# Keys and values side by side in the summing matmuls of a memory-attention and FFN kernel

## The chip, the cores and the metric

The kernel runs on one core of one Trainium2 chip, in one launch. The metric is the device time of that launch in microseconds (us), as the median of repeated runs. A profile is one further execution, recorded instruction by instruction; its span runs from the first to the last instruction of the program.

The engines are named as in the profile: PE (TensorE, matrix multiplication; PEld is its loading of the stationary operand), DVE (VectorE), ACT (ScalarE), POOL (GpSimd) and SP (SyncE, which here issues every DMA).

## The reference: what is computed

For 8 batches of 8 heads, with 576 positions (S), head width 64 (D) and 32 memory slots (M), an attention goes through a small memory. Its output, 4608 rows of 512 columns, then goes through a feed-forward layer of width 2048:

```python
a = softmax(phi, axis=positions)                 # (B, H, S, M)
k_m = einsum('bhsm,bhsd->bhmd', a, k)            # sums over positions
v_m = einsum('bhsm,bhsd->bhmd', a, v)
attn = softmax(q @ k_m.T / sqrt(D), axis=slots)  # (B, H, S, M)
x = concat_heads(attn @ v_m)                     # (B * S, 512)
h = x @ w_in
out = (h * erf(softplus(h))) @ w_out
```

All inputs and outputs are fp32; the feed-forward weights arrive as 64-bit words that the kernel decodes on DVE and ACT.

## The kernel before, in words

**Folding.** The kernel never forms `x`. It multiplies `v_m` with `w_in` first (function `vw`, matmul at L637, tile `psa<-w_in,vm`), so that the first feed-forward matmul (`ffn1`, L737, `psh`) takes the attention weights as its moving operand. A batch has 16 such steps, one per 128 columns of the hidden layer, and each step is followed by softplus and erf on ACT, the product on DVE (`g_split`), and the second feed-forward matmul (`ffn2`, L796, `pso`) some steps later. `ffn1` is split into two halves of 288 positions; from the fifth step on it runs in three products of rounded and rest parts (`at_hi`, `at_lo`, `vw_hi`, `vw_lo`), `ffn2` in the same way from the seventeenth step on. Before that they run as plain fp32 matmuls, each of which shows as two records of PE in the profile.

**The summing matmuls.** `one_memory` (L571 to L627) computes `k_m` and `v_m` of one batch. The 576 positions lie in five pieces of up to 116 rows. For each of two groups of four heads (index `g`), for keys and then for values (`x`), for each piece `c` and for each head `j` of the group, a matmul at L585 (`psa<-kv,phi`) takes the 32 columns of `phi` of that head as the stationary operand and 64 columns of keys or values as the moving one. Head `j` writes the PSUM partitions from 32`j` on, so the four heads of a group stand in four separate quarters of the array's columns. From the second batch on that is one piece of PE's order with 2 x 2 x 5 x 4 = 80 matmuls; in the first batch it is split in two calls, keys and values apart. ACT then scales the sums (`kvk`, L599), PE turns them (L607), and ACT writes them to `km` and `vm`.

**Loads.** `load_kv` (L406) loads one tile of four heads, keys or values: four loads per batch of 640 KB each. They, `phi`, the queries `q` and one weight tile (`wf`) share five buffers of the pool `raw`, so a load of `q` waits for the last reader of a `kv` tile. All loads go through SP's one queue in the order in which SP issues them; in the first 60 us these are mostly the weights (`w<-w_in`, `w<-w_out`, 1024 KB each), which stand in eight buffers of the pool `wo`.

**Decoding weights.** `decode` (L425) turns a loaded weight tile into fp32 in five steps: a clamp on DVE (L432), two scalings on ACT (L438, L442), a merge (L446) and a sign step (L469) on DVE. For `w_in` the sign step writes a tile of its own, and with it the buffer is free for the next load.

**What sets the order.** All operations are first recorded with a cost, a rank and what they read and write. `Plan.order` (L128) then plays them against an estimate of every engine and emits them in the resulting order; each engine executes its list in that order, with semaphores for what really has to wait. For a load the estimate is at L219 to L222: the transfer begins 900 ns after its issue or when the one ahead has landed, goes at 250 to 385 bytes per ns, and is visible 900 ns later. `together` (L538) joins small matmuls to one piece of kind "small"; from the third batch on the sums of a batch and a `vw` piece of the batch before are one such piece.

Of the kernel before, what the change touches and what calls it, by code (L numbers as in the profile page):

```python
# [71 lines left out]
class Plan:  # L72
# [55 lines left out]
    def order(self):  # L128
# [27 lines left out]
        while len(out) < len(self.ops):  # L156
# [62 lines left out]
            if e == SP:  # L219
                begin = max(now + 900, landed)  # L220
                landed = begin + x.nbytes / (250 if x.nbytes < 1.2e5 else 340 if begin < 13000 else 385)
                x.end = landed + 900  # L222
# [17 lines left out]
def tile_memory_attention_then_erf_softplus_ffn(  # L240
    ctx: ExitStack,
    tc: tile.TileContext,
    qT: bass.AP,
    kv: bass.AP,
    phi: bass.AP,
# [23 lines left out]
    ROWS = [min(ROW, S - c * ROW) for c in range(NC)]  # L269
    assert NC == -(-S // ROW) and D < ROWS[-1]  # L270
    RAW = 5
# [45 lines left out]
    def tile_(tag, *key, shape=None, dtype=F32, pool=None):  # L317
        key = plan.tile(tag, *key)
        p, s, d = SHAPES.get(tag, (pool, shape, dtype))
        T[key] = lambda: pools[p].tile(s, d, name=key[0], tag=tag, bufs=BUFS.get(tag))  # L320
        return key
# [83 lines left out]

    def load_kv(rank, b, x, g):  # L406
        key = tile_("raw", "kv", b, x, g, shape=[P, NC, 4 * D], pool="raw")
        load(rank, P * NC * 4 * D * 4, [key],
             lambda: nc.sync.dma_start(out=get(key), in_=kv[b, x, g]))  # L409

# [160 lines left out]
    def one_memory(rank, b, part):  # L571
# [7 lines left out]
        def sums():  # L579
            for n, g in enumerate(gs):  # L580
                for y, x in enumerate(xs):
                    for c, ln in enumerate(ROWS):
                        for j in range(4):
                            h = 4 * g + j
                            nc.tensor.matmul(  # L585
                                out=get(ps)[M * j : M * (j + 1), n, y * D : (y + 1) * D],
                                lhsT=get(a)[:ln, c, h * M : (h + 1) * M],
                                rhs=get(("kv", b, x, g))[:ln, c, j * D : (j + 1) * D],
                                start=(c == 0),
                                stop=(c == NC - 1),  # L590
                            )

# [310 lines left out]
    for b in range(1, B):  # L903
# [4 lines left out]
        when(n, load_phi, at(n - 5), b)  # L908
        for x in range(2):
            for g in range(NG):  # L910
                when(n, load_kv, at(n - 4 + 2 * x + g), b, x, g)
        when(n, memories, at(n), at(n + 3), b, TOGETHER if b == 1 else [])
# [92 lines left out]
```

## Time and profile before

| | before |
|---|---|
| median of 3 runs | 722.64 us (720.65, 722.64, 722.93) |
| profiled execution | 725.49 us |
| its span, first to last instruction | 723.7 us |
| PE busy | 711.9 us (98%) |
| DVE, ACT, POOL busy | 516.4, 433.6, 103.3 us (71%, 60%, 14%) |
| DMA | 66.80 MB, mean 92 GB/s |

A row of the profile reads: line, engine, operation, written tile `<-` read tiles, the shape of the stationary operand (rows*columns) and of the moving one for PE, the count, then busy time and the mean of one in ns. In a timeline the first number is the start in us from the span's start, the second the length of the merged group, and a bracket at the end tells for how long the engine had been idle and what ended that. Matmuls overlap, so the length of one record says less than the distance from one start to the next. "PEclk" in a table of stretches is the share of the full TensorE clock that was granted there.

### The profile page before, as it was taken

What the parts mean: (1) busy time and instruction counts of PE and PEld (TensorE: products, weight loads), DVE (VectorE), ACT (ScalarE), POOL (GpSimd) and SP (SyncE); (2) the same over time, 40 slices, a digit from 0 to 9 for tenths busy, and PEclk for the clock granted to TensorE, in tenths of its full rate; (3) what the DMA queues carried; (4) which work ended last, traced back from release to release, by engine and by line L of the source; (5) the groups of instructions that cost most, each with busy time, mean ns of one, the idle gap of its engine ahead of it and who ended that gap; (6) DMA issues with size and microseconds to landing.
All of it is one profiled execution on the core that took longest, in us unless ns stands there. A gap on an engine that the chain in (4) does not pass through costs nothing.

```text
span 723.7 us, 13374 instructions
## 1 busy us (share of the span) xinstructions
PE 711.9 (98%) x5430; PEld 557.7 (77%) x5430; DVE 516.4 (71%) x950; ACT 433.6 (60%) x642; POOL 103.3 (14%) x262
## 2 busy tenths in 40 slices
PE   8999899999999999999999999999999999999997
PEld 3565555778788887888888888888888888888886
DVE  3999879877965688847974568858885378866630
ACT  4799977966644556654565545755673446664611
POOL 0022102110101111301110112111111011111110
PEclk9999999999999999999999999999999999999999
DMA  9995621171105201062102511053100300010002
GB/s 320 405 404 176 211 81 36 51 254 37 37 1 203 82 33 38 4 236 63 38 1 83 183 54 37 1 205 99 37 1 1 124 16 1 1 45 15 1 0 74
DMA packets 27054, 66.80 MB, mean 92 GB/s; under 512 B 2032, under 2 KB 10224, under 8 KB 25968
## 3 DMA queue, kind: packets, MB, share of 16 engines
q1 hardware_dynamic: 26992, 65.94, 25.9%
q8 instruction: 43, 0.70, 0.4%
q14 instruction: 19, 0.16, 0.1%
HBM read 56.49 MB, written 9.44 MB: 91 GB/s over the span
## 4 chain that ended last, share of the span: by engine, by line
PE 89%; ACT 6%; DMA 3%; SPq 1%; issue 0%; DVE 0%
PE pso L796 48%; PE psh L737 26%; PE psr L796 6%; PE psa L637 6%; DMA q<-qT 3%; PE psa L585 2%; ACT w L442 1%; ACT w L438 1%; ACT e L760 1%; SPq L409 1%; ACT e L765 1%; ACT L760 1%; ACT h L753 0%; PE idle L368 0%; PE psa L607 0%
## 5 line engine op out<-in xcount | busy, mean ns | idle before, releaser
L796 PE MATMUL pso<-wo,g_hi 128*128 128x512 f32 x896 | 281.1, 395 | 0.0
L760 ACT ACTIVATE e<-h 128x576 f32<-128x576 f32 x128 | 87.4, 686 | 178.6 <-DVE h L752 176.6
L796 PEld LDWEIGHTS pso<-wo,g_hi 128*128 128x128 f32 x896 | 160.3, 188 | 42.2 <-issue 15.1
L796 PE MATMUL pso<-wo,g_lo 128*128 128x512 f32 x448 | 176.1, 393 | 0.0
L752 DVE COPY h<-psh 128x288 f32<-128x288 f32 x240 | 107.0, 451 | 48.9 <-PE psh L737 47.2
L737 PE MATMUL psh<-at_hi,vw_hi 128*128 128x288 f32 x496 | 113.6, 310 | 0.0
L792 POOL CAST rest<-g_hi 128x64 fp32r<-128x64 f32 x112 | 49.7, 443 | 406.0 <-DVE g_hi L787 392.2
L737 PE MATMUL psh<-at_lo,vw_hi 128*128 128x288 f32 x496 | 106.6, 297 | 0.0
L737 PE MATMUL psh<-at_hi,vw_lo 128*128 128x288 f32 x496 | 106.3, 296 | 0.0
L785 DVE TENSOR_TENSOR e<-e,h 128x576 f32<-128x576 f32 x112 | 82.8, 751 | 30.3 <-ACT e L765 30.1
L737 PEld LDWEIGHTS psh<-at_hi,vw_hi 128*128 128x128 f32 x496 | 86.5, 189 | 22.1 <-issue 8.2
L796 PEld LDWEIGHTS pso<-wo,g_lo 128*128 128x128 f32 x448 | 84.1, 188 | 19.2
L788 DVE TENSOR_TENSOR g_lo<-e,g_hi 128x576 fp32r<-128x576 f32 x112 | 86.4, 772 | 6.2
L787 DVE CAST g_hi<-e 128x576 fp32r<-128x576 f32 x112 | 50.6, 453 | 46.0 <-PE pso L796 43.4
L765 ACT ACTIVATE e<-e 128x576 f32<-128x576 f32 x128 | 80.3, 675 | 0.4
L737 PEld LDWEIGHTS psh<-at_hi,vw_lo 128*128 128x128 f32 x496 | 80.2, 189 | 0.0
L737 PEld LDWEIGHTS psh<-at_lo,vw_hi 128*128 128x128 f32 x496 | 79.4, 188 | 0.0
L359 DVE TENSOR_TENSOR vw_lo<-psa,vw_hi 128x512 fp32r<-128x512 f32 (+1 forms) x68 | 41.3, 632 | 16.9 <-ACT vw_hi L357 16.7
L796 PE MATMUL pso<-w,g 128*128 128x512 f32 x112 | 52.9, 604 | 0.0
L796 PE MATMUL psr<-wo,rest 128*128 128x512 f32 x192 | 49.0, 391 | 0.0
L357 ACT ACTIVATE vw_hi<-psa 128x512 fp32r<-128x512 f32 (+1 forms) x68 | 34.9, 554 | 22.7 <-PE psa L637 22.7
L792 POOL CAST rest<-g_lo 128x64 fp32r<-128x64 f32 x112 | 34.0, 304 | 90.6 <-DVE g_lo L788 86.4
(80 smaller groups left out, 690.6 us busy)
## 6 DMA issues: line engine op xcount, KB each, us to landing
kv<-kv SPq DMA_DIRECT2D x32, 640.0 KB, 8.0
q<-qT SPq DMA_DIRECT2D x16, 576.0 KB, 6.0
w<-w_in SPq DMA_DIRECT2D x8, 1024.0 KB, 14.2
w<-w_out SPq DMA_DIRECT2D x8, 1024.0 KB, 14.7
out<-ot SPq DMA_DIRECT2D x32, 256.0 KB, 2.1
phiT<-phiT SPq DMA_DIRECT2D x16, 288.0 KB, 3.0
phi<-phi SPq DMA_DIRECT2D x7, 640.0 KB, 7.6
out<-ot SPq DMA_DIRECT2D x8, 128.0 KB, 2.3
```

The costliest lines, as they stand in the source:

```text
L357: lambda: nc.scalar.activation(get_hi(), get_src(), AF.Identity))
L359: lambda: nc.vector.tensor_tensor(out=get_lo(), in0=get_src(), in1=get_hi().bitcast(F32), op=ALU.subtract))
L637: nc.tensor.matmul(out=get(ps[par])[p * M : (p + 1) * M, :], lhsT=w[rows, p, :], rhs=x[rows, p, :], start=True, stop=True,)
L737: nc.tensor.matmul(out=get(ps), lhsT=x[:, g, k % 4 * P : (k % 4 + 1) * P], rhs=y[:, g, :], start=(n + g == 0), stop=(n == len(parts) - 1 a ...
L752: lambda: nc.vector.tensor_copy(out=keep(), in_=get(ps)),
L760: last[:] = [op(ACT, on_act(S), rank, [("h", i)], [e], lambda: nc.scalar.activation(get(e), get(("h", i)), AF.Softplus), kind="softplus", ...
L765: last[:] = [op(ACT, on_act(S), rank, [e], [e], lambda: nc.scalar.activation(get(e), get(e), AF.Erf), kind="erf", edge=edge, after=last)]
L785: op(DVE, on_dve(S), rank, [e, h], [e], lambda: nc.vector.tensor_tensor(out=get(e), in0=get(e), in1=get(h), op=ALU.mult))
L787: op(DVE, on_dve(S, 1), rank, [e], [hi], lambda: nc.vector.tensor_copy(out=get(hi), in_=get(e)))
L788: op(DVE, on_dve(S), rank, [e, hi], [lo], lambda: nc.vector.tensor_tensor(out=get(lo), in0=get(e), in1=get(hi).bitcast(F32), op=ALU.subtract))
L792: lambda x=x, y=y: nc.gpsimd.tensor_copy(out=rest[:, k, x, cols], in_=get(y)[:, NT * P :]))
L796: nc.tensor.matmul(out=o, lhsT=y, rhs=z, start=(start and n == 0), stop=(stop and n == len(parts) - 1))
```

## The change

It has two parts, which are built in together.

**Layout and loops.** Of the first batch, keys and values stay in separate tiles of four heads (`kv_0`). From the second batch on the host lays keys and values of each head side by side, 64 columns of keys and then 64 of values, and a tile holds two heads instead of four heads of one kind. A tile is as large as before, 640 KB, and a batch has four of them as before. In `one_memory` the loop over keys and values is gone: one matmul takes the 128 columns of a head, so 2 x 5 x 4 = 40 matmuls do what 80 did, each twice as wide. The planned cost of the piece is the same as before. The four loads of a batch are recorded with the groups outside and the pairs inside, so that both tiles of the first four heads come first. With the loop over pieces now outside that over heads, both tiles of a group are read until the last of its 20 matmuls.

**Planned loads.** The planner lets a transfer begin 1400 ns after its issue instead of 900.

```diff
             if e == SP:
-                begin = max(now + 900, landed)
+                begin = max(now + 1400, landed)
                 landed = begin + x.nbytes / (250 if x.nbytes < 1.2e5 else 340 if begin < 13000 else 385)
...
     def load_kv(rank, b, x, g):
         key = tile_("raw", "kv", b, x, g, shape=[P, NC, 4 * D], pool="raw")
-        load(rank, P * NC * 4 * D * 4, [key],
-             lambda: nc.sync.dma_start(out=get(key), in_=kv[b, x, g]))
+        src = kv[b - 1, 2 * g + x] if b else kv_0[x, g]
+        load(rank, P * NC * 4 * D * 4, [key], lambda: nc.sync.dma_start(out=get(key), in_=src))
...
             for n, g in enumerate(gs):
-                for y, x in enumerate(xs):
-                    for c, ln in enumerate(ROWS):
-                        for j in range(4):
-                            h = 4 * g + j
-                            nc.tensor.matmul(
-                                out=get(ps)[M * j : M * (j + 1), n, y * D : (y + 1) * D],
-                                lhsT=get(a)[:ln, c, h * M : (h + 1) * M],
-                                rhs=get(("kv", b, x, g))[:ln, c, j * D : (j + 1) * D],
-                                start=(c == 0),
-                                stop=(c == NC - 1),
-                            )
+                for c, ln in enumerate(ROWS):
+                    for j in range(4):
+                        h, w = 4 * g + j, n_x * D
+                        kv_of, at_ = (("kv", b, j // 2, g), j % 2) if b else (("kv", b, xs[0], g), j)
+                        nc.tensor.matmul(
+                            out=get(ps)[M * j : M * (j + 1), n, :w],
+                            lhsT=get(a)[:ln, c, h * M : (h + 1) * M],
+                            rhs=get(kv_of)[:ln, c, at_ * w : (at_ + 1) * w],
+                            start=(c == 0),
+                            stop=(c == NC - 1),
+                        )
...
-        for x in range(2):
-            for g in range(NG):
-                when(n, load_kv, at(n - 4 + 2 * x + g), b, x, g)
+        for g in range(NG):
+            for x in range(2):
+                when(n, load_kv, at(n - 4 + 2 * g + x), b, x, g)
...
-    kv = np.stack([k, v]).reshape(2, B, 2, H // 2, S, D).transpose(1, 0, 2, 4, 3, 5)
+    kv = np.stack([k, v])
...
-        "kv": rows(kv.reshape(B, 2, 2, S, H // 2 * D)),
+        "kv_0": rows(kv[:, 0].reshape(2, 2, H // 2, S, D).swapaxes(2, 3).reshape(2, 2, S, H // 2 * D)),
+        "kv": rows(kv[:, 1:].reshape(2, B - 1, H // 2, 2, S, D).transpose(1, 2, 4, 3, 0, 5)
+                   .reshape(B - 1, H // 2, S, 4 * D)),
```

Few places of the engines' orders differ, the first of them in the second batch. (The changed kernel's lines are 1 to 2 higher: L585 became L587, L637 L639, L737 L739, L796 L798.) The first place is PE where the second batch is prepared. `pso<-w,g` is an `ffn2` matmul in plain fp32, `psa<-w_in_103,vm_98` a `vw` piece of the first batch. Before:

```order
L737 MATMUL psh<-at_hi,vw_lo 128x288 x2
L796 MATMUL pso<-w,g 128x512
L637 MATMUL psa<-w_in_103,vm_98 32x256 x8
L796 MATMUL pso<-w,g 128x512 x3
L737 MATMUL psh<-at_hi,vw_hi 128x288 x2
```

In the changed kernel:

```order
L739 MATMUL psh<-at_lo,vw_hi 128x288 x2
L739 MATMUL psh<-at_hi,vw_lo 128x288 x2
L639 MATMUL psa<-w_in_103,vm_98 32x256 x8
L798 MATMUL pso<-w,g 128x512 x4
L739 MATMUL psh<-at_hi,vw_hi 128x288 x2
```

The `vw` piece stands ahead of one `ffn2` matmul that it stood behind. Twelve `ffn1` matmuls later, at the sums of the second batch (`psa<-kv,phi`), PE before:

```order
L737 MATMUL psh<-at_hi,vw_lo 128x288 x2
L796 MATMUL pso<-w,g 128x512 x2
L585 MATMUL psa<-kv,phi 32x64 x80
L637 MATMUL psa<-w_in_103,vm_98 32x256 x8
L796 MATMUL pso<-w,g 128x512
L607 MATMUL psa<-ident,kvk 128x128 x4
```

And now:

```order
L739 MATMUL psh<-at_hi,vw_lo 128x288 x2
L798 MATMUL pso<-w,g 128x512
L587 MATMUL psa<-kv,phi 32x128 x40
L639 MATMUL psa<-w_in_103,vm_98 32x256 x8
L798 MATMUL pso<-w,g 128x512 x2
L609 MATMUL psa<-ident,kvk 128x128 x4
```

The 80 matmuls became 40 of twice the width, and one `ffn2` matmul went from ahead of them to behind them. Between the `vw` piece and the sums stand as many `ffn2` matmuls as before, five.

The third place is DVE over both of these stretches, before. `w` is a weight tile being decoded, with the sign step of `w_in_103` at L469; `pmx` the maxima of the third batch's `phi`, `h` a copy of an `ffn1` half out of PSUM, `vw_lo` the rest part of a `vw` piece.

```order
L494 TENSOR_REDUCE pmx<-phiT 128x1 x2
L446 SCALAR_TENSOR_TENSOR w<-w 128x1024
L752 COPY h<-psh 128x288
L469 SCALAR_TENSOR_TENSOR w_in_103<-w 128x4x256
L446 SCALAR_TENSOR_TENSOR w<-w 128x1024
L496 TENSOR_SCALAR pmx<-pmx 128x1
L469 SCALAR_TENSOR_TENSOR w<-w 128x1024
L359 TENSOR_TENSOR vw_lo<-psa,vw_hi 128x256 x2
L496 TENSOR_SCALAR pmx<-pmx 128x1
L446 SCALAR_TENSOR_TENSOR w<-w 128x1024
L432 TENSOR_SCALAR w<-w 128x1024
L469 SCALAR_TENSOR_TENSOR w_in_103<-w 128x4x256
```

And in the changed kernel:

```order
L496 TENSOR_REDUCE pmx<-phiT 128x1
L448 SCALAR_TENSOR_TENSOR w<-w 128x1024
L754 COPY h<-psh 128x288
L471 SCALAR_TENSOR_TENSOR w_in_103<-w 128x4x256
L448 SCALAR_TENSOR_TENSOR w<-w 128x1024
L754 COPY h<-psh 128x288
L471 SCALAR_TENSOR_TENSOR w<-w 128x1024
L360 TENSOR_TENSOR vw_lo<-psa,vw_hi 128x256 x2
L496 TENSOR_REDUCE pmx<-phiT 128x1
L448 SCALAR_TENSOR_TENSOR w<-w 128x1024
L498 TENSOR_SCALAR pmx<-pmx 128x1
L471 SCALAR_TENSOR_TENSOR w_in_103<-w 128x4x256
```

One of the two maxima left the place ahead of the first sign step of `w_in_103`, and the clamp of another weight (L432) left the place ahead of the second; one copy of `h` came in from ACT. SP issues its loads in the same sequence of kinds as before. The other places move `ffn2` steps by one past neighbours: the sums of the third batch stand one `ffn2` step of three matmuls later than before, and in three places near the ends of later batches an `ffn2` step changes place with `ffn1` halves.

More of the change, by code (lines that the diff above doesn't have):

```diff
@@ L243, in tile_memory_attention_then_erf_softplus_ffn @@
     qT: bass.AP,
+    kv_0: bass.AP,
     kv: bass.AP,
@@ L269, in tile_memory_attention_then_erf_softplus_ffn @@
     ROWS = [min(ROW, S - c * ROW) for c in range(NC)]
-    assert NC == -(-S // ROW) and D < ROWS[-1]
+    assert NC == -(-S // ROW) and D < ROWS[-1] and H == 8
     RAW = 5
```

## The prediction, made before the changed kernel ran

> **What bounds the kernel now.** I read the page's first part, then the stretches with the granted clock, then PE's waits, and at last PE's timeline around each wait. The page:
>
> ```profile
> PE 711.9 (98%) x5430; PEld 557.7 (77%) x5430; DVE 516.4 (71%) x950; ACT 433.6 (60%) x642; POOL 103.3 (14%) x262
> q8 instruction: 43, 0.70, 0.4%
> ```
>
> The stretches (start:end; then busy time and count of PE, PEld, DVE, ACT, POOL; granted clock, DMA share, GB/s):
>
> ```profile
> 88.30:90.17 1.87, 0.16 (x3) 0.04 (x2) 1.18 (x3) 1.86 (x4) 0.56 (x1) 1.00 1.05 394
> 91.60:95.40 3.80, 3.80 (x25) 1.85 (x23) 2.94 (x6) 1.00 (x2) 0.56 (x2) 0.58 0.75 261
> 95.40:149.00 53.60, 53.60 (x257) 34.58 (x250) 46.85 (x75) 44.72 (x62) 10.11 (x18) 1.00 0.16 52
> 154.00:700.00 546.00, 545.71 (x4112) 454.36 (x4101) 384.58 (x737) 302.69 (x445) 77.84 (x210) 1.00 0.18 60
> ```
>
> After 154 us PE never stops (545.71 of 546.00 us), while DVE is busy for 70% of that and ACT for 55%. There only less work on PE shortens the program, and moving an `ffn2` step past `ffn1` halves costs nothing, hidden by that slack. The waits that an order can change lie ahead of 154 us. Two matter.
>
> **The sums.** PE's timeline at the fourth batch's sums, and the groups of the sums and of the 128-column turns:
>
> ```profile
> 222.50 2.45 PE L585 MATMUL psa<-kv,phi 116*32 116x64 f32 x160
> 224.88 1.09 PE L637 MATMUL psa<-w_in,vm 64*32 64x512 f32 x16
> 225.90 0.50 PE L796 MATMUL pso<-wo,g_hi 128*128 128x512 f32 x1
> 228.99 0.60 PE L607 MATMUL psa<-ident,kvk 128*128 128x128 f32 x4
> L585 PE MATMUL psa<-kv,phi 116*32 116x64 f32 x1024 | 19.0, 220 | 1.4 <-DMA kv<-kv 1.4
> L607 PE MATMUL psa<-ident,kvk 128*128 128x128 f32 x32 | 5.4, 281 | 0.0
> ```
>
> The 80 matmuls are 160 records, two passes each. The piece takes 224.88 - 222.50 = 2.38 us; with 0.22 us for the last record's length (220 ns), the pace is (2.45 - 0.22) / 159 = 14.0 ns per record, or 56 ns for the four that stand side by side in the array's quarters. Is this the time of 64 columns, or of issuing an instruction? The turns stream 128 columns and follow each other at (0.60 - 0.28) / 3 = 107 ns (0.28 us is one record's length, 281 ns in its group). Half of it is 53 ns. So the columns set the pace, with some 3 ns per pass on top. Forty matmuls are 20 rounds of four records at 107 to 110 ns, 2.14 to 2.20 us, against 40 rounds x 56 = 2.24. That saves 0.04 to 0.10 us per piece, and there are seven. I take **0.5 us**; the bounds are 0 (a round exactly twice as long) and 7 x (2.38 - 2.14) = 1.7 us, if the piece's ends shrink too.
>
> [...]
>
> The layout itself I cost at nothing: the loads are as large and as many, and PE's 1.4 us of waiting for `kv` tiles, told by the last row but one above, is these two waits of the first batch, whose loads don't change:
>
> ```profile
> 8.73 0.77 PE L585 MATMUL psa<-kv,phi 116*32 116x64 f32 x40 [0.54 <-DMA kv<-kv]
> 10.36 0.77 PE L585 MATMUL psa<-kv,phi 116*32 116x64 f32 x40 [0.86 <-DMA kv<-kv]
> ```
>
> No later sums waited for a tile: the loads are ahead of them, which covers their new order. Without that lead a tile would cost its lateness at the sums.
>
> **The gap in the third batch's sums.** PE, and the chain of waits there:
>
> ```profile
> 149.58 2.46 PE L585 MATMUL psa<-kv,phi 116*32 116x64 f32 x160
> 151.97 0.61 PE L637 MATMUL psa<-w_in,vm 64*32 64x512 f32 x1
> 153.37 1.09 PE L637 MATMUL psa<-w_in,vm 64*32 64x512 f32 x15 [0.79 <-issue]
> 154.39 0.74 PE L796 MATMUL pso<-wo,g_hi 128*128 128x512 f32 x2
> 152.58 0.79 issue
> q8 instruction: 1, 0.02, 4.1%
> ```
>
> The `vw` piece behind the sums takes 154.39 - 151.97 = 2.42 us here, and 225.90 - 224.88 = 1.02 us a batch later: 1.40 us lost after its first record, to nothing that the profile shows as a wait. The last row is from the DMA view of 150.5 to 152.5 us: one piece of instructions was on its way. The page has 43 of them with 0.70 MB, 16 KB each; PE's 10,860 matmuls and loads of weights make 253 per piece. Sums and `vw` piece together are 320 + 32 = 352 instructions in 2.4 us, more than one piece, so PE can run dry. In the changed kernel they are 160 + 32 = 192, less than a piece. I take the whole **1.4 us**, bounds 0 and 1.4.
>
> [...]
>
> **The wait for q.** PE, SP and DVE in the second batch:
>
> ```profile
> 74.21 1.02 PE L796 MATMUL pso<-w,g 128*128 128x512 f32 x2
> 75.39 0.67 PE L637 MATMUL psa<-w_in,vm 64*32 64x256 f32 x16 [0.16 <-ACT e L760]
> 80.25 1.88 PE L796 MATMUL pso<-w,g 128*128 128x512 f32 x4
> 82.06 2.46 PE L585 MATMUL psa<-kv,phi 116*32 116x64 f32 x160
> 88.03 0.43 PE L737 MATMUL psh<-at_hi,vw_lo 128*128 128x288 f32 x2
> 90.17 0.84 PE L637 MATMUL psa<-q,km 64*32 64x288 f32 x16 [1.71 <-DMA q<-qT]
> 81.86 0.33 SPq L391 DMA_DIRECT2D w<-w_out  x1
> 82.89 0.94 SPq L414 DMA_DIRECT2D q<-qT  x2
> 82.89 7.14 DMA q<-qT
> q<-qT SPq DMA_DIRECT2D x1, 576.0 KB, 4.4
> 71.21 1.40 DVE L494 TENSOR_REDUCE pmx<-phiT 128x1 f32<-128x576 f32 x2
> 74.03 1.21 DVE L469 SCALAR_TENSOR_TENSOR w_in<-w 128x1024 int32<-128x1024 int32 x1
> 79.95 0.70 DVE L432 TENSOR_SCALAR w<-w 128x1024 f32<-128x1024 f32 x1 [0.37 <-DMA w<-w_out]
> 80.56 1.22 DVE L469 SCALAR_TENSOR_TENSOR w_in<-w 128x1024 int32<-128x1024 int32 x1
> 76.54 0.69 ACT L357 ACTIVATE vw_hi<-psa 128x256 fp32r<-128x256 f32 x2
> 77.06 1.24 ACT L442 ACTIVATE w<-w 128x1024 f32<-128x1024 f32 x1
> 80.18 1.27 ACT L515 ACTIVATE phi<-phi 116x1280 f32<-116x1280 f32 x1
> ```
>
> PE is through with `ffn1` at 88.03 + 2 x 0.13 = 88.29 and gets `q` at 90.17: 1.88 us idle. `q` takes 7.14 us to land, but 4.4 us when nothing is ahead of it (the DMA view of its issue at 223.4 us). Ahead of it is a `w_out` load, issued at 81.86, when the sign step of `w_in` ends (80.56 + 1.22 = 81.78) and frees its buffer. That step stands behind a clamp that waits 0.37 us for a load and takes 0.61 us. The change puts the clamp behind it and a copy of 0.4 us ahead: the `w_out` load goes out 0.37 + 0.61 - 0.4, with a small step gone some 0.7 us earlier, and `q` lands 0.7 us earlier, since the queue is what it waits for.
>
> Does PE come to it later? The first sign step loses one maximum of 0.70 us ahead of it, so the `vw` piece starts about 0.6 us earlier, at 74.8, though PE then idles 0.6 us ahead of it instead of 0.3: the `ffn2` matmul of 74.21, which filled that time, now follows. ACT rounds this piece ahead of a weight's scaling instead of behind it (76.54, ended by 77.2); it can do so from about 75.6, when it used to copy `h`, so the scaling of 77.06 and the exponentials at 80.18 keep their times. The sums follow the `vw` piece 82.06 - 75.39 = 6.67 us later as before, at 81.5, or 81.6 when the exponentials (80.18 + 1.27) are through. PE's way from there to `q` is 88.29 - 82.06 = 6.23 us, plus 0.9 for the `ffn2` matmul put there (two took 82.06 - 80.25 = 1.81), less 0.07 for the sums: 88.7. `q`'s first buffer is free after 18 of 40 matmuls instead of 20 of 80, 0.4 us later in the piece, which the earlier start gives back. So `q` lands at 90.03 - 0.7 and the piece starts at 89.5: **0.7 us** gained, bounds 0 and 90.17 - 88.7 = 1.5. What is late next is nothing on PE: 95.40 to 149 is filled.
>
> **The clock behind it.** Between 91.60 and 95.40 us the clock is 0.58: 3.80 x 0.42 = 1.6 us lost, right behind the idle 1.88 us, and nowhere else in the quoted stretches. With 0.8 us idle I expect full clock. But one profile can't say how often the timed runs had the drop; they spread over 2.3 us, more than it costs. I take half, **0.8 us**, bounds 0 and 1.6.
>
> **The sum.** 0.5 + 1.4 + 0.7 + 0.8 = 3.4 us. The profiled execution took 725.49 (span 723.7 and 1.8 around it), which would become 722.1; the median of the runs is 2.85 us lower, so I take 722.64 - 3.4 = **719.2 us**.
>
> **Rivals.**
> *One: only the sums shrink.* DVE meets another wait (its merges wait for ACT), `w_out` goes out as before, idle time and clock stay, and the gap moves elsewhere: 722.1 us. For it: moved steps elsewhere in a full order change nothing. Against: the clamp's wait is in the trace. Chance 0.16.
> *Two: the gap at 152 us stays*, because it isn't instructions: 719.2 + 1.4 = 720.6. For it: one gap in seven batches. Against: no wait ends there, and a piece was in flight. Chance 0.20.
> *Three: issue sets the sums' pace.* Then 80 records take 80 x 14.0 = 1.1 us, 1.2 less in each of seven: 711.5. Against it, the turns' 107 ns. Chance 0.03.
> *Four, slower: the `vw` piece put forward waits.* If the first sign step ends at 75.24 as before, PE idles 0.9 us more at 74.2; if `w_out` then goes out no earlier, `q` comes 0.4 us later by its buffer and the idle time grows to about 3.2 us in two parts. From about 1.9 us on the clock drops, and a second stretch of 1.6 us is lost: 722.64 - 0.5 + 1.3 + 1.6 = 725.0, with the gap unchanged. Chance 0.06.
>
> **How the numbers follow.** The forecast has 0.55. A measurement of this kernel tells about 0.3% from no change, 2.2 us, so faster means below 720.5: 0.85 of the forecast, half of rival two and rival three, 0.60. Slower by that, above 724.8: most of rival four, 0.05. The rest, 0.35, is no change. The range starts where all terms have their upper bounds but the sums' (722.64 - 0.5 - 1.4 - 1.5 - 1.6 = 717.6) and reaches to 722.3, past rival one.
>
> **What would show it.** The sums' piece 2.3 us from start to start with 80 records; the `vw` piece behind the third batch's sums in one group of 16; instructions in 38 pieces; the `w_out` load ahead of `q` issued near 81.2, PE's `q` piece near 89.5, and a granted clock of 1.00 behind it. Wrong would be: sums of 1.2 us or of more than 2.4; the gap still there; a longer bracket at the `q` piece.

## The result and the profile after

The changed kernel takes **718.97 us** (median of 5 runs, 717.89 to 719.05) against 722.64 us before: 0.9943 of the time, 95% interval 0.9923 to 0.9963. A second measurement on another occasion gave 0.9950 (0.9937 to 0.9964). Its profiled execution took 717.89 us, with a span of 716.1 us. The prediction was 719.2 us.

The page of the changed kernel, engines and instruction pieces:

```profile
PE 708.0 (99%) x4870; PEld 555.7 (78%) x4870; DVE 516.9 (72%) x951; ACT 432.8 (60%) x641; POOL 105.8 (15%) x262
q8 instruction: 38, 0.62, 0.4%
```

PE's timeline after the change, at the sums of the third batch and at those of the fifth:

```profile
145.70 2.40 PE L587 MATMUL psa<-kv,phi 116*32 116x128 f32 x80
148.03 1.09 PE L639 MATMUL psa<-w_in,vm 64*32 64x512 f32 x16
149.05 0.74 PE L798 MATMUL pso<-wo,g_hi 128*128 128x512 f32 x2
...
298.90 2.40 PE L587 MATMUL psa<-kv,phi 116*32 116x128 f32 x80
301.23 1.09 PE L639 MATMUL psa<-w_in,vm 64*32 64x512 f32 x16
302.25 0.53 PE L739 MATMUL psh<-at_hi,vw_hi 128*128 128x288 f32 x2
```

The sums take 148.03 - 145.70 = 2.33 us from start to start, 2.38 before. The `vw` piece behind them is one group of 16 and takes 1.02 us, where it took 2.42 us before: that gap is gone. The fifth batch holds something that the prediction had overlooked. The same place in the kernel before, and its view of PE's waits (line and releaser, then us in total, times, longest):

```profile
304.99 2.45 PE L585 MATMUL psa<-kv,phi 116*32 116x64 f32 x160
307.37 1.06 PE L637 MATMUL psa<-w_in,vm 64*32 64x512 f32 x7
308.72 1.07 PE L637 MATMUL psa<-w_in,vm 64*32 64x512 f32 x9 [0.29 <-issue]
309.71 0.53 PE L737 MATMUL psh<-at_hi,vw_hi 128*128 128x288 f32 x2
```

```profile
PE psa L637 <- issue: 1.1, 2, 0.8
```

There was a second gap: 309.71 - 307.37 = 2.34 us instead of 1.02, 1.32 us lost, though the bracket shows only 0.29 us of it, because the group of seven ahead is drawn with 1.06 us, up to 308.43, which covers the rest. The waits said "2 times". The changed kernel has neither gap.

The wait for `q` in the second batch, PE after the change:

```profile
86.16 0.43 PE L739 MATMUL psh<-at_hi,vw_lo 128*128 128x288 f32 x2
87.07 0.92 PE L639 MATMUL psa<-q,km 64*32 64x288 f32 x16 [0.48 <-DMA q<-qT]
```

0.48 us of idle time by the bracket, 1.71 before.

Where the time went is read from the starts of PE's pieces in its timelines. The last two columns are a second profile of each kernel, told of below:

| start of PE's piece, us | before | after | before, again | after, again |
|---|---|---|---|---|
| third `w_in,vm` piece | 43.32 | 41.79 | 43.45 | 43.73 |
| second batch's sums | 82.06 | 79.58 | 82.20 | 81.54 |
| second batch's first `q` piece | 90.17 | 87.07 | 90.80 | 88.92 |
| a `w_in,vm` piece past the third batch's sums | 182.64 | 176.63 | 181.41 | 178.40 |
| a `w_in,vm` piece past the fifth batch's sums | 331.19 | 323.73 | 329.78 | 325.81 |
| end of PE | 719.25 | 711.46 | 718.03 | 713.53 |

The first pair differs by 7.8 us at the end, twice what the medians differ by. 1.53 us of it arise in the first 43 us, where both kernels do the same, and 1.7 us are the half-clock stretch that the prediction quoted (3.41 us at 0.50, from 91.38 to 94.79 us). In the second pair no half-clock stretch falls behind the first row. It differs by 4.50 us at the end, or by 4.78 us counted from the first row, where the changed kernel is 0.28 us later (a half-clock stretch at 11.4 us of its profile lies ahead of that row).

### The profile page after: what moved, and what is told of

The parts are those of the page before. It is cut to its first block, busy times and chain, and to the rows that moved or that the text cites. A ratio compares the mean times of both kernels' runs of the same rounds, so it can differ in the third digit from the quotient of the medians.

```text
span 716.1 us, 12256 instructions
## 1 busy us (share of the span) xinstructions
PE 708.0 (99%) x4870; PEld 555.7 (78%) x4870; DVE 516.9 (72%) x951; ACT 432.8 (60%) x641; POOL 105.8 (15%) x262
## 4 chain that ended last, share of the span: by engine, by line
PE 89%; ACT 6%; DMA 3%; SPq 1%; DVE 0%; issue 0%
PE pso L798 49%; PE psh L739 26%; PE psr L798 6%; PE psa L639 5%; DMA q<-qT 3%; PE psa L587 2%; ACT w L444 1%; ACT w L440 1%; ACT e L762 1%; ACT e L767 1%; ACT L762 1%; ACT h L755 0%; SPq L411 0%; PE idle L369 0%; PE psa L609 0%
## 5 line engine op out<-in xcount | busy, mean ns | idle before, releaser
L798 PE MATMUL pso<-wo,g_hi 128*128 128x512 f32 x896 | 280.8, 395 | 0.0
L798 PEld LDWEIGHTS pso<-wo,g_hi 128*128 128x128 f32 x896 | 160.2, 188 | 42.1 <-issue 15.1
L798 PE MATMUL pso<-wo,g_lo 128*128 128x512 f32 x448 | 175.9, 393 | 0.0
L739 PE MATMUL psh<-at_hi,vw_hi 128*128 128x288 f32 x496 | 112.8, 309 | 0.0
L739 PE MATMUL psh<-at_lo,vw_hi 128*128 128x288 f32 x496 | 106.2, 296 | 0.0
L739 PE MATMUL psh<-at_hi,vw_lo 128*128 128x288 f32 x496 | 105.9, 295 | 0.0
L739 PEld LDWEIGHTS psh<-at_hi,vw_hi 128*128 128x128 f32 x496 | 86.1, 188 | 21.7 <-issue 7.6
L798 PEld LDWEIGHTS pso<-wo,g_lo 128*128 128x128 f32 x448 | 84.1, 188 | 19.5
L739 PEld LDWEIGHTS psh<-at_hi,vw_lo 128*128 128x128 f32 x496 | 79.8, 189 | 0.0
L739 PEld LDWEIGHTS psh<-at_lo,vw_hi 128*128 128x128 f32 x496 | 79.0, 188 | 0.0
L798 PE MATMUL pso<-w,g 128*128 128x512 f32 x112 | 52.2, 599 | 0.0
L798 PE MATMUL psr<-wo,rest 128*128 128x512 f32 x192 | 49.0, 390 | 0.0
L794 POOL CAST rest<-g_lo 128x64 fp32r<-128x64 f32 x112 | 34.2, 305 | 87.9 <-DVE g_lo L790 85.9
```

Of the source, the lines that this page charges most:

```text
L739: nc.tensor.matmul(out=get(ps), lhsT=x[:, g, k % 4 * P : (k % 4 + 1) * P], rhs=y[:, g, :], start=(n + g == 0), stop=(n == len(parts) - 1 a ...
L794: lambda x=x, y=y: nc.gpsimd.tensor_copy(out=rest[:, k, x, cols], in_=get(y)[:, NT * P :]))
L798: nc.tensor.matmul(out=o, lhsT=y, rhs=z, start=(start and n == 0), stop=(stop and n == len(parts) - 1))
```

## The experiments

### Both kernels once more, and each part of the change alone

Four kernels ran beside the kernel before. The first is that kernel unchanged. The second has the planner's number alone:

```diff
-                begin = max(now + 900, landed)
+                begin = max(now + 1400, landed)
```

The third is the changed kernel with that line set back. The fourth is the changed kernel, in its order and with its layout, with each wide matmul issued as two:

```diff
-                for c, ln in enumerate(ROWS):
-                    for j in range(4):
+                for y in range(n_x):
+                    for c, ln in enumerate(ROWS):
+                        for j in range(4):
...
-                            out=get(ps)[M * j : M * (j + 1), n, :w],
+                                out=get(ps)[M * j : M * (j + 1), n, y * D : (y + 1) * D],
...
-                            rhs=get(kv_of)[:ln, c, at_ * w : (at_ + 1) * w],
+                                rhs=get(kv_of)[:ln, c, at_ * w + y * D : at_ * w + (y + 1) * D],
```

What was expected of the kernel before, again:

> The kernel before, unchanged, for a second profile of it. Theory (the two gaps belong to the program, the start and the clock to the single execution): the vw piece behind the third batch's sums again takes 2.4 us and that behind the fifth batch's 2.3 us instead of 1.02; the start of the w_in,vm piece that stood at 43.32 us moves by up to 1.5 us, since in the changed kernel it stood at 41.79 with the same work ahead of it; the idle time ahead of the second batch's q piece is 1.3 to 1.9 us. Rival (the changed kernel's start is 1.5 us earlier because the first batch's keys and values come from a tensor of their own): that piece stands at 43.3 again, within 0.3 us. The half-clock stretch of 1.6 us behind the q piece: if the idle time sets it, it is there again; if it is a matter of the single execution, it may be gone.

Of the planner's number alone:

> The kernel before with the planner's 1400 in place of 900 and nothing else: the changed order with 80 matmuls of 64 columns per sums. Theory: both gaps stay (2.4 and 2.3 us for the vw pieces behind the third and the fifth batch's sums, 43 pieces of instructions), the idle time ahead of the second batch's q piece falls from 1.7 to about 0.5 us: 0.6 to 1.2 us less than before, 721.4 to 722.0, and up to 1.6 us less again if the timed runs of before had the half-clock stretch. Rival (the gap at 152 us is not a matter of instructions, the moved ffn2 step or loads took it away): both gaps are gone here too, 719.3.

Of the wide sums in the old order:

> The changed kernel with the planner's 900: 40 matmuls of 128 columns per sums in the old order. Theory: both gaps gone (1.02 us for the vw pieces, 38 pieces of instructions) and 0.05 us less in each of seven sums: 2.7 + 0.35 = 3.1 us less than before, 719.6; the idle time ahead of the second batch's q piece stays at 1.3 to 1.9 us. Rival (gaps not a matter of instructions): they stay, 0.35 us less than before, 722.3.

Of narrow sums in the new order and layout:

> The changed kernel, its layout, loads and order, but each summing matmul of 128 columns issued as two of 64, so that sums and vw piece are 352 instructions again. Theory: the gaps are back behind the third and the fifth batch's sums (the stream up to there has as many instructions as before, within 6), each sums takes 2.38 us: 2.7 + 0.35 = 3.1 us more than the changed kernel, 722.0. Rival (the gaps belonged to the order or to the loads): no gap, 719.3.

Measured, as ratios to the kernel before with 95% intervals:

| | narrow sums | wide sums |
|---|---|---|
| old order | 0.9993 (0.9975 to 1.0011) | 0.9950 (0.9934 to 0.9966) |
| new order | **1.0061** (1.0044 to 1.0079) | 0.9943 (0.9923 to 0.9963) |

Narrow sums in the new order with the new layout have 1.0063 (1.0047 to 1.0079), the same as with the old layout: the layout itself costs and gives nothing, the number of matmuls does. The wide sums give the whole gain, also in the old order. The planner's number, for which 1.5 us had been forecast, gives nothing that can be told beside wide sums with PE's instructions as they lie here, and with narrow sums it makes the kernel **slower** by 0.6%, which neither theory nor rival had.

The kernel before, again, in PE's timeline, behind the third and the fifth batch's sums:

```profile
151.05 0.61 PE L637 MATMUL psa<-w_in,vm 64*32 64x512 f32 x1
152.12 1.09 PE L637 MATMUL psa<-w_in,vm 64*32 64x512 f32 x15 [0.46 <-issue]
153.14 0.74 PE L796 MATMUL pso<-wo,g_hi 128*128 128x512 f32 x2
...
306.14 2.19 PE L637 MATMUL psa<-w_in,vm 64*32 64x512 f32 x16
308.26 0.54 PE L737 MATMUL psh<-at_hi,vw_hi 128*128 128x288 f32 x2
```

Both gaps are there again, 1.07 and 1.10 us. Its start is at 43.45 us, that of the wide sums in the old order at 43.27: the early start of the changed kernel's first profile was that execution's own.

The clock, in stretches of the first and of the second profile of the kernel before (start:end; busy time and count of PE, PEld, DVE, ACT, POOL; granted clock, DMA share, GB/s):

```profile
88.00:91.30 3.30, 1.59 (x21) 0.85 (x20) 1.70 (x5) 3.27 (x5) 0.78 (x2) 1.00 1.05 403
91.40:94.80 3.40, 3.40 (x16) 1.86 (x22) 2.54 (x6) 1.20 (x2) 0.56 (x2) 0.50 0.88 312
```

```profile
88.00:91.30 3.30, 1.03 (x21) 0.62 (x19) 1.55 (x4) 3.25 (x6) 0.86 (x3) 1.00 1.04 384
91.40:94.80 3.40, 3.40 (x33) 1.69 (x26) 3.09 (x6) 1.45 (x3) 0.56 (x2) 1.00 0.94 334
```

The second has the longer idle time (2.27 us by its bracket, against 1.71) and no half clock behind it. So the length of the wait alone doesn't decide.

And this is what the new order does to narrow sums. PE in the second batch with the planner's number alone:

```profile
80.75 2.15 PE L585 MATMUL psa<-kv,phi 116*32 116x64 f32 x137
86.64 0.79 PE L585 MATMUL psa<-kv,phi 116*32 116x64 f32 x23 [3.75 <-issue]
87.36 1.11 PE L637 MATMUL psa<-w_in,vm 64*32 64x256 f32 x16
```

The sums stop at the 137th of 160 records for 3.75 us, and again nothing ended the wait that the profile shows. Narrow sums in the new layout do the same (4.03 us). In the third batch both have a gap of 1.6 us, in the fifth one of 1.2.

### What decides where a gap comes

Counting PE's matmuls, loads of weights and semaphore instructions from the program's start puts the gaps in a row. In the kernel before they begin at records 2496 and 5056, with the planner's number at 1472, 2496 and 5056. Each of these is 256 n + 448 (n = 4, 8, 18). The 16 KB pieces of instructions in the DMA records come once per 256 such records, in quiet stretches soonest when PE is at record 256 n + 152. From 448 - 152 = 296 I estimate that a piece is asked for some 300 records ahead of its use. No record shows the asking; a time that an expectation gives for it is an estimate too, that of PE's record 256 n + 148 (record 1428, at 83.62 us, in the kernel before). In the kernel before, the sums use up 300 records in 2.07 us at the fastest; in the changed kernel no 300 records in a row take less than 10 us behind the first 40 us. From the record at 256 n + 148 to PE's going on, the four gaps of the kernel before's two profiles took 3.65, 3.51, 3.31 and 3.30 us.

If that is the cause, instructions that do nothing, put in front, move the gaps. The kernel issues matmuls on zeros during PE's first waits; some of these were issued as four of 128 columns instead of one of 512, so that each adds six instructions (a load of weights and a matmul, three times) and no columns:

```diff
-            nc.tensor.matmul(
-                out=idle[0].rearrange("p (n c) -> p n c", c=P), lhsT=zeros,
-                rhs=zeros.unsqueeze(1).to_broadcast([P, DM // P, P]), start=True, stop=True,
-            )
+            n_parts = 4 if len(idle) <= 11 else 1
+            idle.append(None)
+            w = DM // P // n_parts
+            for y in range(n_parts):
+                nc.tensor.matmul(
+                    out=idle[0].rearrange("p (n c) -> p n c", c=P)[:, y * w : (y + 1) * w], lhsT=zeros,
+                    rhs=zeros.unsqueeze(1).to_broadcast([P, w, P]), start=True, stop=True,
+                )
```

With 11 of them, 66 instructions, the kernel before was expected so:

> The kernel before with 66 more small instructions on PE in its first microseconds (11 of the matmuls that fill PE's waits there are issued as four of 128 columns each), the order otherwise unchanged. Theory: PE's instructions come in pieces of 256; a piece is asked for 300 instructions before it is needed, and it takes 3.3 to 3.7 us; PE stands still where those 300 are used up faster. With 66 more ahead the boundary moves to other places: the gaps behind the third and the fifth batch's sums go (1.02 us for these vw pieces), and gaps of 1.2 to 1.4 us come behind or in the fourth and the eighth batch's sums, near 224 and 561 us; the time stays within 0.3% of before. Rival (the gaps belong to these two places: their loads, tiles or buffers): they stay in the third and the fifth batch, and none comes elsewhere.

Measured: 1.0054 (1.0034 to 1.0073). PE's timeline at the fourth, fifth and eighth batch's sums:

```profile
225.06 1.04 PE L641 MATMUL psa<-w_in,vm 64*32 64x512 f32 x2
226.30 1.09 PE L641 MATMUL psa<-w_in,vm 64*32 64x512 f32 x14 [0.19 <-issue]
227.31 0.73 PE L800 MATMUL pso<-wo,g_hi 128*128 128x512 f32 x2
...
308.75 1.09 PE L641 MATMUL psa<-w_in,vm 64*32 64x512 f32 x16
309.77 0.40 PE L741 MATMUL psh<-at_hi,vw_hi 128*128 128x288 f32 x1
...
559.66 2.34 PE L589 MATMUL psa<-kv,phi 116*32 116x64 f32 x152
563.75 0.32 PE L589 MATMUL psa<-kv,phi 112*32 112x64 f32 x8 [1.75 <-issue]
564.00 1.09 PE L641 MATMUL psa<-w_in,vm 64*32 64x512 f32 x16
```

The fifth batch's gap is gone (1.02 us), and gaps stand in the fourth (1.23 us lost) and the eighth (564.00 - 559.66 = 4.34 us instead of 2.38, 1.96 lost), the two batches that had been named. So the gaps belong to PE's instruction count, not to the place, its tiles or its loads. The time was missed, +0.5% where no change was forecast: the eighth batch's gap is longer than 1.4 us, 0.58 us stay in the third, and this profile has a half-clock stretch behind `q`. None of its six timed executions has a mean granted clock above 0.998, so that stretch is probably in most of them.

With 22 split, 132 instructions, in two kernels:

> The order of the changed kernel with the narrow sums, as the run with the planner alone, and 132 more small instructions on PE in the first microseconds. Theory: none of the boundaries then falls into the second, third or fifth batch's sums; the stall of 3.75 us in the second, the 1.6 us in the third and the 1.2 us in the fifth are gone, one gap of about 1.3 us comes at the seventh batch's sums near 472 us. 3.75 + 1.6 + 1.2 - 1.3 = 5.2 us less than with the planner alone, and about 1.7 us more where that run had a half-clock stretch: 0.2 to 0.5% faster than before. Rival (the 3.75 us belong to the moved order: a tile or a load that the sums wait for): the stall in the second batch stays, and the kernel stays 0.4 to 0.6% slower than before.

> The changed kernel with the same 132 instructions more. Theory: with wide sums no place in the program uses up 300 instructions in less than 3.7 us, so the boundary may lie anywhere: no gap of 0.6 us or more behind 60 us, 0.994 to 0.995 of before like the changed kernel. Rival (the changed kernel was only lucky with where its boundaries fall): a gap of 1 us or more somewhere, 0.996 or more.

The new order with narrow sums goes from 1.0061 to **0.9960** (0.9945 to 0.9975), by nothing but 132 instructions that compute nothing. Its sums in the second and in the seventh batch:

```profile
81.21 2.46 PE L589 MATMUL psa<-kv,phi 116*32 116x64 f32 x160
83.59 0.66 PE L641 MATMUL psa<-w_in,vm 64*32 64x256 f32 x16
...
468.32 2.46 PE L589 MATMUL psa<-kv,phi 116*32 116x64 f32 x160
472.32 1.09 PE L641 MATMUL psa<-w_in,vm 64*32 64x512 f32 x16 [1.54 <-issue]
```

The stall of the second batch is gone, and the one gap stands at the seventh batch's sums as forecast (472.32 - 468.32 is 1.62 us more than 2.38). The changed kernel with the same 132 has 0.9939 (0.9922 to 0.9956). No wait in its view of PE's waits is put down to `issue`: with wide sums no stall came with the pieces ending at this place either.

### Why 3.75 us in the second batch

The gaps of the kernel before cost 1.1 to 1.4 us, this one 3.75. At 80.3 us a `w_out` load is issued; it was left out:

```diff
+                if c == NPR - 1:
+                    nc.gpsimd.memset(t.bitcast(F32), 0.0)
+                    return
                 nc.sync.dma_start(
                     out=t.rearrange("p (r d) -> p r d", d=DM), in_=w_out[:, 2 * c : 2 * c + 2]
                 )
```

> The run with the planner alone, but the last w_out load, which is issued near 80.3 us, is left out, and its buffer is filled with zeros by POOL instead (so one eighth of w_out counts as zero). Theory (the piece of instructions asked for at 78.2 us came 8.5 us later instead of 3.5 because it stood behind this load in the DMA engines): the piece is there by 82.2 us and the stall in the second batch's sums falls from 3.75 us to under 0.6 us; 3.2 to 5 us less than with the planner alone. The gaps in the third and the fifth batch stay. Rival (the stall's length has nothing to do with loads): it stays at 3 us or more.

Measured: 1.0000 (0.9985 to 1.0016), 4.7 us less than the planner's number alone by the medians (723.80 and 728.53 us). Not all of that is the stall: the two profiled executions, each with one half-clock stretch, are only 1.6 us apart (725.39 and 727.02 us), and the mean granted clock of the timed ones is 0.998 to 1.000 here and 0.991 to 0.998 there. And the stall is 1.89 us, not under 0.6:

```profile
80.44 2.15 PE L588 MATMUL psa<-kv,phi 116*32 116x64 f32 x137
84.48 0.54 PE L588 MATMUL psa<-kv,phi 116*32 116x64 f32 x23 [1.89 <-issue]
```

The piece went into the DMA engines at 81.57 us instead of 84.31, 1.1 us behind the start of the sums instead of 3.6, so the load did hold it up by some 2.4 us. It didn't go at 79 us, though, when the engines had nothing to do. My guess was that it had not been asked for by then, which no record shows. In the order before, the second batch's sums stand four records later in the stream (they begin at record 1202, here at 1198), and their piece came at 79.75 us, ahead of them. That gave the last experiment: six instructions more, one split matmul.

> The run with the planner alone (narrow sums in the new order) with 6 more small instructions on PE in its first microseconds: one of the matmuls that fill PE's waits is issued as four. In the order before, the second batch's sums stood 4 instructions later in PE's stream than in the new one, and the piece of instructions that they need came at 79.8 us, ahead of them; in the new order it came at 84.3 us, and PE stood still for 3.75 us. Theory (the place in the stream that asks for the piece lies just behind the sums' first instruction in the new order, so that it is asked for when the sums start and then waits behind a load; a few instructions earlier it is asked for before them): with 6 more the piece comes ahead of the sums, near 79 us, and the stall in the second batch is gone; the gaps in the third and the fifth batch stay (1.2 to 1.6 us each), since their boundaries move by 6 of 256 only. 0.999 to 1.002 of before, where the planner alone had 1.006. Rival (the stall belongs to the new order and its loads): it stays, 1.005 or more.

Measured: **0.9973** (0.9959 to 0.9987), against 1.0061 without them. PE in the second batch, and the DMA queues from 77.9 to 79.9 us:

```profile
80.47 2.45 PE L589 MATMUL psa<-kv,phi 116*32 116x64 f32 x160
82.85 0.66 PE L641 MATMUL psa<-w_in,vm 64*32 64x256 f32 x16
83.44 1.98 PE L800 MATMUL pso<-w,g 128*128 128x512 f32 x4
```

```profile
q8 instruction: 1, 0.02, 4.0%
```

The piece came at 78.3 us and the stall is gone, while the third batch keeps its gap. Six empty instructions are worth 0.9% here, 6.7 us by the medians of the two occasions. The clock has a part in that beside the stall: its mean is 0.999 or more in all twelve executions, and 0.998 or less in all six without the six instructions. With the sums' first instruction at record 1024 + 174, the piece came behind their start, by 3.6 us and, without the load, by 1.1 us; with it at 1024 + 178 (the order before) and at 1024 + 180 (six more), the piece came 2.3 and 2.2 us ahead of their start. Why these few records decide isn't shown: the packet can be seen, the request can't.

### What shortened the wait for q

Wide sums in the old order had 0.55 us of idle time ahead of the `q` piece, where 1.3 to 1.9 had been expected, though their `w_out` load went out at 82.26 us, later than before (81.86). So the order, to which the prediction had put the gain, isn't needed for a short wait. In the two profiles of before a piece of instructions passed through the DMA engines at 87.9 and 87.4 us, while `q` was on its way; with wide sums in the old order none did. 132 instructions bring one back among these loads (22 matmuls split, as above):

> Wide sums in the old order (the run with the new layout alone) with 132 more small instructions on PE in its first microseconds. In the old order with wide sums no piece of instructions was asked for between 62 and 89 us, and q landed 2.2 us behind the w_out load ahead of it; in the two profiles of before a piece was asked for at 83.6 to 83.8 us, its 16 KB came at 87.4 to 87.9 us, and q landed 3.5 and 4.1 us behind w_out. With 132 more, a piece is asked for at 83.7 us again. Theory (the wait for q in before was 1 to 1.9 us longer because a piece of instructions came through the DMA engines while w_out and q did): w_out and q together are 1 us or more later again, the idle time ahead of the second batch's q piece goes from 0.55 us back to 1.3 us or more; no gap of 0.6 us behind it; 0.996 to 0.998 of before. Rival (the wide sums shortened the wait for q in another way): idle time of 0.4 to 0.8 us, 0.994 to 0.996 of before.

> The changed kernel, unchanged, for a second profile and beside the run with wide sums in the old order. Theory (its start at 41.8 us for the third w_in,vm piece was the single execution's): the piece stands at 42.6 to 43.6 us, as in the other profiles, and the span is 716 to 718.5 us; no gap of 0.6 us behind 60 us. It has 0.993 to 0.995 of before; wide sums in the old order had 0.995, so the order's share is at most 0.2%.

PE's `q` piece, and the loads issued and queues at work from 83.5 to 88.3 us, in the wide kernel of the old order without and then with the 132 (of a load: KB, then median us to landing):

```profile
89.21 0.84 PE L639 MATMUL psa<-q,km 64*32 64x288 f32 x16 [0.55 <-DVE h L754]
```

```profile
q<-qT SPq DMA_DIRECT2D x2, 576.0 KB, 5.8
```

```profile
89.89 0.84 PE L643 MATMUL psa<-q,km 64*32 64x288 f32 x16 [1.68 <-DMA q<-qT]
```

```profile
q8 instruction: 1, 0.02, 1.2%
...
q<-qT SPq DMA_DIRECT2D x2, 576.0 KB, 7.0
```

The idle time is 1.68 us again. From the issue of `w_out` to the start of the `q` piece it takes 89.89 - 82.02 = 7.87 us with the piece of instructions among the loads, and 89.21 - 82.26 = 6.95 without: 0.9 us more. The other 0.2 us of the difference are PE's, which comes to `q` that much sooner after the issue. The piece is one packet, and it took 0.9 us too (1.2% of 16 engines' 4.8 us).

In the changed kernel, though, a piece passed among these loads as well, at 83.4 us and in its second profile at 85.3 us, and the wait is short all the same. Its second profile, in DVE, SP, the DMA queues from 83.5 to 88.3 us, and PE:

```profile
79.74 1.23 DVE L471 SCALAR_TENSOR_TENSOR w_in<-w 128x1024 int32<-128x1024 int32 x1
81.03 0.33 SPq L392 DMA_DIRECT2D w<-w_out  x1
81.67 0.69 DVE L434 TENSOR_SCALAR w<-w 128x1024 f32<-128x1024 f32 x1
...
q8 instruction: 1, 0.02, 1.3%
...
88.92 0.84 PE L639 MATMUL psa<-q,km 64*32 64x288 f32 x16 [0.37 <-DVE g L776]
```

`w_out` goes out when the sign step ends (79.74 + 1.23 = 80.97 us), with the clamp behind it, as the prediction had it. The parts of the wait in ten profiles, all in us, read from the starts of the sums, of the `w_out` load and of the `q` piece with its bracket (in the other three the stall in the sums let `q` land before PE came to it):

| profiles | `w_out` issued before the sums start | sums' start to PE being ready for `q` | `w_out` issued to `q` piece | idle |
|---|---|---|---|---|
| old order, a piece among the loads: before, again, with 66, wide with 132 | 0.20, 0.27, -1.05, 0.05 | 6.39, 6.33, 6.51, 6.13 | 8.31, 8.87, 7.87, 7.87 | 1.71, 2.27, 2.42, 1.68 |
| old order, no piece: wide | 0.27 | 6.13 | 6.95 | 0.55 |
| new order, a piece: changed, again, with 132 | 0.48, 0.51, 0.49 | 7.01, 7.02, 6.98 | 7.97, 7.89, 7.76 | 0.48, 0.37, 0.28 |
| new order, a piece, narrow: with 132, with 6 | 0.48, 0.49 | 7.05, 7.05 | 7.70, 8.88 | 0.17, 1.34 |

The idle time is the third number less the first two. In all ten the piece starts 0.13 to 0.14 us behind `q`'s landing, also where the bracket names DVE. The first two numbers, which go mostly with the order, give the new order 0.9 us in either pair of before and changed (0.28 + 0.62 and 0.24 + 0.69). The third gives these pairs 0.34 and 0.98 us, with a piece among the loads on both sides, at another place; without a piece it is 0.8 to 1.9 us lower than with one. So the order or a missing piece is enough for a short wait, and in the changed kernel no piece is missing.

Over the whole the wide kernel of the old order with the 132 has 0.9990 (0.9976 to 1.0003), slower than the 0.996 to 0.998 expected. One reason is a wait that nobody had forecast, in ACT's and PE's timelines:

```profile
317.17 0.60 ACT L845 ACTIVATE ot<-pso 128x512 f32<-128x512 f32 x1 [1.35 <-DMA out<-ot]
...
317.82 0.72 PE L802 MATMUL pso<-wo,g_hi 128*128 128x512 f32 x2 [1.03 <-ACT ot L845]
```

ACT there waits 1.35 us for a store of the output to land before it frees a PSUM buffer, and PE 1.03 us for ACT. A piece of instructions passed at 305.84 us, among the loads queued ahead of this store, and the store took 8.2 us to land; without the 132 the pieces came at 301.92 and 313.59 us, and it took 5.6 us. That the piece delayed the store fits, but wasn't tried by itself.

The changed kernel, again, has 0.9950 and 0.37 us ahead of `q`; its third `w_in,vm` piece stood at 43.73 us, 0.1 us beyond what was expected. At 0.9950 against 0.9950 for wide sums in the old order, the order's part can't be told from nothing. With the 132 instructions it can: 0.9939 (0.9922 to 0.9956) in the new order against 0.9990 in the old, on two occasions. So what the order is worth depends on where the pieces of instructions fall.

## Why the prediction came out

The number was right, 719.2 against 718.97 us, and the causes of its terms hold in the main. The sizes don't: the gaps and the wait for `q` were put too low and the clock too high for a pair of profiles without the half-clock stretch, so that the agreement to 0.2 us is in part luck.

**Sums, 0.5 us.** Measured 2.38 to 2.33 us in each of seven, 0.35 us: mis-sized slightly. The reason holds: 80 records at (2.40 - 0.27) / 79 = 27 ns are 108 ns per four, with 107 to 110 forecast, against 56 ns for 64 columns, so columns set the pace. Rival three, issue at 14 ns, would have gained 1.2 us per piece.

**The gap, 1.4 us.** The cause, instructions, is shown by the moved gaps, and rival two, that it stays, is out. Two things in this step were wrong. The rule was not that 352 instructions are more than one piece and 192 are less: sums and `vw` piece were 352 instructions in all seven batches and only two had a gap. What goes with a gap is how fast 300 records pass (2.07 us at the fastest in the kernel before, over 10 us in the changed one) and where they lie against 256 n + 448. And there were two gaps, so that the term should have been 2.7 us by that profile; by the second one it is 2.2. "After 154 us PE never stops", read from 545.71 busy us of 546.00, missed the second, because the 1.06 us with which the seven matmuls ahead are drawn cover all but 0.29 us of it. The line `issue: 1.1, 2, 0.8` had it.

Of the 43 pieces of instructions in the kernel before, 41 came without such a gap. Where PE stood still, it cost 0.6 to 4 us here.

**The wait for q, 0.7 us.** The idle time fell by 1.23 us in the first pair and 1.90 in the second, and the step behind it, that the `w_out` load goes out 0.7 us earlier and `q` lands earlier with it, holds in the changed kernel. Counted from the third `w_in,vm` piece, `w_out` goes out 1.2 us earlier in both pairs, so that the step was sized too small. What the prediction left out is that the time in the queue isn't fixed: from the issue of `w_out` to the `q` piece it went from 8.31 to 7.97 us and from 8.87 to 7.89, and it was 6.95 us where no piece of instructions passed.

**The clock, 0.8 us.** The stretch is gone in the changed kernel's profile (1.00 from 60 to 700 us), 1.7 us. But rival four's "From about 1.9 us on the clock drops" doesn't hold: 2.27 us of idle time in the second profile of the kernel before had no half clock behind it (1.00 from 91.4 to 94.8 us). Of 74 executions of the kernel before that were timed beside these runs, 21 had a mean granted clock of 0.997 or less, and their median is 2.4 us above that of the others (725.4 and 723.0 us). 21/74 of 2.4 us is 0.7 us, near the half that was taken. It is a lower count: the profile of the planner's number alone has one such stretch and a mean of 0.998.

**The sum.** In the second pair of profiles, of the 4.78 us counted from the third `w_in,vm` piece, the `q` piece starts 2.16 us earlier, the gaps are 1.07 + 1.10 us, and six more sums 0.30: 4.6 us. Against this the forecast of 3.4 us has 0.8 too little for the gaps, 1.4 too little up to `q`, 0.8 too much for the clock and 0.2 for the sums. The medians differ by 3.4 to 3.7 us, less than these profiles; why is open, though both profiled executions of the kernel before (725.49 and 724.27 us) lie above the median of their occasion. What was missed altogether is that the planner's number, taken alone, costs 4.4 us. Rival four had the sign and the batch, but another mechanism, and in the change as a whole the wide sums take it away.

## What to carry to other kernels

Where an engine works through hundreds of short instructions in a few microseconds, look for idle time put down to "issue" and count the instructions up to it: here the remainder was the same at every gap (256 n + 448), instructions that compute nothing moved the gaps, and halving the instructions there took away 2.2 to 2.7 us of gaps beside 0.35 us of execution time. When an edit of the order gains or loses a few us, run it once more with some empty instructions ahead, since six of them moved the kernel with narrow sums in the new order by 0.9%. And run the halves of a change apart: here one half costs 0.6% alone and nothing beside the other, until the instructions shift.

## What was not expected of the hardware

- Stalls of PE that end with nothing the profile shows came only at record 256 n + 448 of its stream: 19 of over 0.55 us in eight profiles with narrow sums, none in five with wide ones. In 15 of the 19 PE went on 3.3 to 4.1 us after record 256 n + 148; in the second batch's stall, with a 1 MB load ahead, it took 5.9 us from the sums' start (80.75 to 86.64 us).
- With one 16 KB piece of instructions among `w_out` and `q`, `q` came 0.8 to 1.9 us later (6.95 us from the issue of `w_out` in the one profile without a piece, 7.70 to 8.88 in the nine with one). Only the 132 instructions test this by themselves: 0.9 us.
- The half-clock stretch of the kernel before lasted 3.41 us (0.50 from 91.38 to 94.79 us), behind 1.71 us of idle time by the bracket. With the planner's number alone it is about 3.4 us (clock 0.57 from 86.6 to 88.0 us and 0.67 from 88.0 to 91.3), with a stall of 3.75 us; in the narrow kernel of the new layout about 6.8 us (0.70, 0.50 and 0.62 from 86.6 to 88.0, 88.0 to 91.3 and 91.4 to 94.8), with one of 4.03 us. The wait of 2.27 us in the second profile of the kernel before has none behind it. What sets such a stretch isn't shown.
